# Linear attention and a multiplicative FFN on one core: full-height matmuls with block-diagonal kv, phi as a min, batch 0's attention ahead of the weights, and a new order on every engine

## The chip, the cores and the metric

One core of one Trainium2 chip. The metric is device time in microseconds of one execution, the median of several; the four runs of the kernel before lie within 0.6%, those of the changed kernel within 0.8%. The profile is of one further execution. It names the engines PE (TensorE), PEld (TensorE weight load), DVE (VectorE), ACT (ScalarE), POOL (GpSimd) and SP (SyncE). A ratio below is the mean time of one kernel's fast runs over that of the kernel before's fast runs of the same rounds, so not quite the ratio of the medians quoted beside it.

## The reference

```python
# q, k, v: (8 batches, 8 heads, 576 positions, 64), fp32
phi = lambda x: np.where(x > 0, x, np.exp(x) - 1.0) + 1.0
kv  = einsum('bhsd,bhse->bhde', phi(k), v)
z   = phi(k).sum(axis=2)
x   = einsum('bhsd,bhde->bhse', phi(q), kv) / (einsum('bhsd,bhd->bhs', phi(q), z)[..., None] + 1e-6)
x   = x.transpose(0, 2, 1, 3).reshape(4608, 512)
out = ((x @ w1) * (x @ w2)) @ w3 @ w_out     # 512 -> 1024 -> 1024 -> 512
```

Both kernels fold `w3 @ w_out` into one "fused weight" (wf) and cut the 4608 rows of x into nine chunks of 512. A chunk is eight a/b products (13.8 us of TensorE) and four outputs (6.9 us). 576 positions are 4 x 128 plus a remainder of 64.

## The kernel before

Every engine runs a fixed list of steps; the order of the lists is written out by hand. The parts that matter, shortened (`...` marks a cut):

```python
def phi_exp(name, b, g):                    # ScalarE
    nc.scalar.activation(out=e, in_=x, func=AF.Exp)
def phi_min(name, b, g):                    # VectorE
    nc.vector.tensor_scalar_min(out=e, in0=e, scalar1=1.0)
def phi_max(name, b, hp):                   # VectorE: max(x + 1, min(exp x, 1))
    nc.vector.scalar_tensor_tensor(out=out, in0=x, scalar=1.0, in1=e, op0=ALU.add, op1=ALU.max)

def kv_half(b, g):                          # 64-row matmuls, two halves side by side
    ...
    for n, (kk, vv, halves) in enumerate(steps):
        for r in halves:
            rows = slice(r * R, (r + 1) * R)
            nc.tensor.matmul(kvp[:, r, i * W:(i + 1) * W], kk[rows], vv[rows], ...)
    nc.scalar.copy(out=kvf, in_=kvp[:, 0, 0:2 * W])
    nc.vector.tensor_tensor(out=kvs[b]..., in0=kvf, in1=kvp[:, 1, 0:2 * W], op=ALU.add)
# numerators: 64-row matmuls, one per head (u) and head pair (hp)
nc.tensor.matmul(nd[0:n, u, hp * (D + 1):(hp + 1) * (D + 1)], w[rows], kvs[b][rows, hp, u, :], ...)
# transposes of q and x: on TensorE for the first batches, by DMA for q of batches 4 to 7, x of 2 and 4 to 7
nc.sync.dma_start(out=dst, in_=src, transpose=True)
```

## Time and profile before

| | kernel before |
|---|---|
| time, median | 261.6 us (260.9 to 262.5) |
| profiled span | 258.1 us, mean clock 0.999 |
| kv of batch 1, of batch 7 | 46.4 us, 193.1 us |
| all loads of the start (weights, batches 0 and 1) landed | about 56 us |

How to read it: the start is bound by loads. After that TensorE is full up to the end. The prediction shows the rows.

The table by stretches gives one line for 60 to 185 us, in which most of the attention of batches 2 to 7 is loaded and worked (in the kernel before, batch 7's comes after it); it is the line that all the rest is compared with. DMA share is the packets' time over that of 16 engines; it can pass 1, and is no proof of a bound by itself: from 50 to 75 us, in the prediction's table, it is 1.06 while TensorE is busy 24.95 of 25 us.

```profile
core 0: us, PE busy (x) PEld busy (x) DVE busy (x) ACT busy (x) POOL busy (x), PEclk, DMA share, GB/s
60.00:185.00 125.00, 124.47 (x943) 60.20 (x952) 104.52 (x282) 72.16 (x119) 2.45 (x4) 1.00 0.86 223
```

TensorE is busy 124.47 of 125 us at full clock, DMA at 0.86. The waits of TensorE in this stretch are an empty list.

### The profile page before, as it was taken

What the parts mean: (1) busy time and instruction counts of PE and PEld (TensorE: products, weight loads), DVE (VectorE), ACT (ScalarE), POOL (GpSimd) and SP (SyncE); (2) the same over time, 40 slices, a digit from 0 to 9 for tenths busy, and PEclk for the clock granted to TensorE, in tenths of its full rate; (3) what the DMA queues carried; (4) which work ended last, traced back from release to release, by engine and by line L of the source; (5) the groups of instructions that cost most, each with busy time, mean ns of one, the idle gap of its engine ahead of it and who ended that gap; (6) DMA issues with size and microseconds to landing.
All of it is one profiled execution on the core that took longest, in us unless ns stands there. A gap on an engine that the chain in (4) does not pass through costs nothing.

```text
span 258.1 us, 4507 instructions
## 1 busy us (share of the span) xinstructions
PE 237.4 (92%) x1656; PEld 116.2 (45%) x1673; DVE 167.9 (65%) x426; ACT 129.0 (50%) x205; POOL 21.1 (8%) x42
## 2 busy tenths in 40 slices
PE   1138999999999999999999999999999999999994
PEld 1124554545454454455444444444444444444442
DVE  0025787969978979997968589468866543423320
ACT  2048587858478664677353645726533203331421
POOL 8000765000101000000000000000000000000000
PEclk9999999999999999999999999999999999999999
DMA  6999999999898599939988975934980124003024
GB/s 100 200 257 378 316 229 245 208 334 307 302 291 250 87 340 215 307 104 253 211 193 245 369 160 123 248 99 131 218 220 26 34 57 124 0 37 125 3 82 163
DMA packets 70085, 48.98 MB, mean 190 GB/s; under 512 B 34416, under 2 KB 64368, under 8 KB 70064
## 3 DMA queue, kind: packets, MB, share of 16 engines
q1 hardware_dynamic: 63104, 42.54, 61.4%
q0 software_dynamic: 6816, 6.03, 14.1%
q8 instruction: 13, 0.21, 0.3%
q10 hardware_dynamic: 144, 0.13, 0.1%
q14 instruction: 8, 0.07, 0.1%
HBM read 38.80 MB, written 9.44 MB: 187 GB/s over the span
## 4 chain that ended last, share of the span: by engine, by line
PE 84%; DMA 8%; ACT 2%; SPq 1%; issue 1%; DVE 1%; DVEq 0%; POOLq 0%
PE a_ps L371 25%; PE b_ps L371 24%; PE o_ps L390 23%; DMA k<-in_k_dram 4%; DMA w3b<-in_moe_w_dram 4%; PE kvp L199 3%; PE wf_ps L464 3%; PE nd L265 3%; SPq L111 1%; PE tp L309 1%; PE w3p L454 1%; PE xtp L285 1%; PE o_ps L417 1%; DVE qj L162 1%; ACT e L137 0%
## 5 line engine op out<-in xcount | busy, mean ns | idle before, releaser
L371 PEld LDWEIGHTS <-w_sb 128*128 128x128 bf16 x576 | 54.2, 98 | 63.4 <-issue 0.5
L377 DVE TENSOR_TENSOR ab<-a_sb,b_ps 128x512 bf16<-128x512 f32 x72 | 49.0, 684 | 46.6 <-PE b_ps L371 35.4
L371 PE MATMUL a_ps<-xt,w_sb 128*128 128x512 bf16 x288 | 75.1, 380 | 0.1
L371 PE MATMUL b_ps<-xt,w_sb 128*128 128x512 bf16 x288 | 74.9, 379 | 0.0
L376 ACT COPY a_sb<-a_ps 128x512 f32<-128x512 f32 x72 | 41.9, 586 | 56.8 <-PE a_ps L371 55.6
L390 PE MATMUL o_ps<-wf_sb,ab 128*128 128x512 bf16 x266 | 63.2, 379 | 0.7
L390 PEld LDWEIGHTS <-ab 128*128 128x128 bf16 x280 | 26.7, 98 | 30.8
L393 ACT COPY o_sb<-o_ps 128x512 f32<-128x512 f32 x24 | 14.0, 583 | 30.7 <-PE o_ps L390 30.7
L162 DVE SCALAR_TENSOR_TENSOR kj<-k,e 128x256 bf16<-128x256 f32 x64 | 23.6, 417 | 0.1
L162 DVE SCALAR_TENSOR_TENSOR qj<-q,e 128x256 bf16<-128x256 f32 x64 | 23.4, 417 | 0.1
L141 DVE TENSOR_SCALAR e<-e 128x1024 bf16<-128x1024 bf16 x32 | 13.4, 420 | 14.2 <-ACT e L137 14.2
L137 ACT ACTIVATE e<-q 128x1024 bf16<-128x1024 f32 x16 | 16.7, 1058 | 9.3 <-DMA q<-in_q_dram 9.1
L454 PE MATMUL w3p<-ident,w3b 128*128 128x128 bf16 x64 | 6.1, 253 | 15.0 <-ACT w3t L455 8.0
L137 ACT ACTIVATE e<-k 128x1024 bf16<-128x1024 f32 x16 | 16.9, 1056 | 4.1 <-DMA k<-in_k_dram 2.7
L275 DVE TENSOR_TENSOR xn<-nd,r 128x512 bf16<-128x512 f32 x28 | 18.0, 686 | 0.0
L464 PE MATMUL wf_ps<-wo_sb,w3t 128*128 128x512 bf16 x61 | 16.7, 412 | 1.0 <-ACT w3t L455 0.8
L454 PEld LDWEIGHTS <-w3b 128*128 128x128 bf16 x64 | 4.9, 113 | 16.6 <-DMA w3b<-in_moe_w_dram 8.2
L393 DVE COPY o_sb<-o_ps 128x512 f32<-128x512 f32 x11 | 7.6, 688 | 6.4 <-PE o_ps L390 6.4
L171 ACT CAST vt<-v 128x1024 bf16<-128x1024 f32 x9 | 9.3, 1046 | 2.0 <-DMA v<-in_v_dram 2.0
L203 ACT COPY kvf<-kvp 128x260 f32<-128x260 f32 x14 | 5.3, 375 | 8.9 <-PE kvp L199 8.7
L464 PEld LDWEIGHTS <-w3t 128*128 128x128 bf16 x64 | 6.2, 104 | 7.8 <-issue 1.7
L199 PE MATMUL kvp<-vt,kj 64*128 64x130 bf16 x224 | 9.2, 217 | 0.0
(81 smaller groups left out, 163.5 us busy)
## 6 DMA issues: line engine op xcount, KB each, us to landing
out_dram<-o_sb SPq DMA_DIRECT2D x31, 256.0 KB, 3.2
k<-in_k_dram SPq DMA_DIRECT2D x7, 1024.0 KB, 8.6
q<-in_q_dram SPq DMA_DIRECT2D x7, 1024.0 KB, 8.2
v<-in_v_dram SPq DMA_DIRECT2D x6, 1024.0 KB, 7.4
w3b<-in_moe_w_dram POOLq DMA_DIRECT2D x8, 256.0 KB, 7.1
v<-in_v_dram SPq DMA_DIRECT2D x4, 512.0 KB, 8.5
w_sb<-in_moe_w_dram POOLq DMA_DIRECT2D x8, 256.0 KB, 11.3
out_dram<-o_sb SPq DMA_DIRECT2D x9, 128.0 KB, 2.4
```

The costliest lines, as they stand in the source:

```text
L137: nc.scalar.activation(out=e, in_=x, func=AF.Exp)
L141: nc.vector.tensor_scalar_min(out=e, in0=e, scalar1=1.0)
L162: nc.vector.scalar_tensor_tensor(out=out, in0=x, scalar=1.0, in1=e, op0=ALU.add, op1=ALU.max)
L199: nc.tensor.matmul(kvp[:, r, i * W:(i + 1) * W], kk[rows], vv[rows], start=(n == 0), stop=(n == (NJ if r == g else NJ - 1)))
L275: nc.vector.tensor_tensor(out=dst.rearrange("p (c u) e -> p u c e", u=2), in0=v4[:, :, :, 0:D], in1=r[0:n].unsqueeze(3).to_broadcast([n, 2 ...
L371: nc.tensor.matmul(ps, w[:, kc, f * P:(f + 1) * P], xt[:, 4 * c:4 * c + 4, kc, :], start=(kc == 0), stop=(kc == KC - 1))
L376: nc.scalar.copy(out=a_sb, in_=a_ps)
L377: nc.vector.tensor_mul(out=abs_[c][:, f, :], in0=a_sb, in1=b_ps)
L390: nc.tensor.matmul(o_ps, ab[:, f, m * P:(m + 1) * P], wf_sb[:, f, :], start=(f == 0), stop=(f == FC - 1))
L393: copy_of(alt)(out=o_sb, in_=o_ps)
L454: nc.tensor.transpose(tp[:, kc, :], raw["w3", i][:, kc * P:(kc + 1) * P], ident)
L464: nc.tensor.matmul(wfs[i], w3ts[i][:, kc, :], wo_sb[:, kc, :], start=(kc == 0), stop=(kc == FC - 1))
```

## The change

Intent: matmuls of one shape only (128 rows) so that TensorE never changes its tiling; less VectorE work for phi; an earlier first product, by loading batch 0 ahead of the weights. The diff is long; its core, cut:

```diff
-        nc.vector.tensor_scalar_min(out=e, in0=e, scalar1=1.0)
-            nc.vector.scalar_tensor_tensor(out=out, in0=x, scalar=1.0, in1=e, op0=ALU.add, op1=ALU.max)
+        nc.vector.tensor_scalar(out=d, in0=raw, scalar1=0.0, scalar2=1.0, op0=ALU.max, op1=ALU.add)
+        nc.vector.tensor_tensor(out=phi, in0=d, in1=e, op=ALU.min)      # min(exp x, max(x, 0) + 1)

-    def kv_half(b, g): ...                       # 36 matmuls of 64 rows a batch, copy and add
+    def kv(b, hp):                               # 5 matmuls of 128 rows a head pair
+        for j in range(NJ):
+            nc.tensor.matmul(dst, kj[:, hp, j]..., vt[:, j, 2 * hp:2 * hp + 2, :]..., ...)
+        nc.tensor.matmul(dst, kr[:, ...], vrz[:, b % 2, ...], ...)   # remainder, other batch's rows zero in vrz
+    def kc(b, g0, ng, r, eng):                   # the diagonal blocks alone go to kvb; the rest of kvb stays zero
+        copy_of[eng](out=kvb[b % 3][rows, ..., r, :], in_=ps["kv", b][rows, ..., r, :])
+    def na(b, jp, g):                            # numerators: 128 rows x 130 columns, two heads at once
+        nc.tensor.matmul(o[:, i, ...], sb["qt", b][:, hp, ...], kvb[b % 3][:, hp]..., start=True, stop=True)

+    # DMA transposes: q and x of batches 2 to 7 (six of each)
-    ORDER = """ L0.3 E0 I0 M0.0 x0.2 N0.3 E1 X0.0 w0 ...      (w3 and w_out first)
+    ORDER = """ ... lr:k,0,s ld:k,0,0,4,s lr:v,0,s ld:v,0,0,4,s ld:q,0,0,4,s ...   (batch 0, w1/w2, w_out, w3, batch 1)
```

In the step names of the new order, `ld`/`lr` are loads (whole batches and remainders), `x`, `t`, `m` the three steps of phi, `kv`/`kc` kv and its copies, `na`/`nd` numerators and division, `qt`/`qc` and `xp`/`xc` transposes on TensorE with their copies, `qd` and `xd` transposes by DMA, `f`, `ac`, `ab` the a/b products, `o`, `oc`, `st` output, copy, store, `w3t`, `wf` the fused weight.

> **What bounds the kernel now.** I read the page's table by slices first, then the chain that ended last, the table by stretches, the order of time on TensorE, and last the landings of the DMAs.
>
> The page:
>
> ```profile
> span 258.1 us, 4507 instructions
> PE 237.4 (92%) x1656; PEld 116.2 (45%) x1673; DVE 167.9 (65%) x426; ACT 129.0 (50%) x205; POOL 21.1 (8%) x42
> PE   1138999999999999999999999999999999999994
> DVE  0025787969978979997968589468866543423320
> PEclk9999999999999999999999999999999999999999
> DMA  6999999999898599939988975934980124003024
> PE 84%; DMA 8%; ACT 2%; SPq 1%; issue 1%; DVE 1%; DVEq 0%; POOLq 0%
> ```
>
> TensorE is full from the fourth slice (a slice is 6.45 us) to the end at an ungated clock. Only the first three slices and the tail are not TensorE; there the DMA row is at 9. So the kernel is a start of some 30 us, a solid block of matmuls, and a tail. The table by stretches says the same:
>
> ```profile
> core 0: us, PE busy (x) PEld busy (x) DVE busy (x) ACT busy (x) POOL busy (x), PEclk, DMA share, GB/s
> 20.00:30.00 10.00, 9.11 (x61) 4.89 (x59) 7.24 (x18) 8.36 (x11) 4.71 (x8) 1.00 1.10 368
> 50.00:75.00 25.00, 24.95 (x180) 12.67 (x180) 22.65 (x60) 16.95 (x29) 1.22 (x2) 1.00 1.06 301
> 75.00:100.00 25.00, 24.89 (x207) 12.46 (x207) 20.73 (x56) 16.16 (x27) 1.22 (x2) 1.00 0.94 218
> 100.00:125.00 25.00, 24.89 (x227) 12.38 (x227) 23.55 (x70) 16.06 (x27) 0.00 (x0) 1.00 0.90 234
> ```
>
> From 50 to 125 us TensorE is 99.6% busy although VectorE is 89% busy (66.9 of 75) and DMA 0.90 to 1.06: both have little room beneath TensorE.
>
> A busy PE may hide gaps, so I took start-to-start times from the timeline. An a/b product is 8 matmuls in 1.73 us, 216 ns each; a 128x128 transpose costs 57.5 ns. The small attention products:
>
> ```profile
> 74.66 1.03 PE L371 MATMUL b_ps<-xt,w_sb 128*128 128x512 bf16 x4
> 75.62 0.40 PE L199 MATMUL kvp<-vt,kj 64*128 64x130 bf16 x8
> 76.36 0.44 PE L199 MATMUL kvp<-vt,kj 64*128 64x130 bf16 x9
> 76.59 0.22 PE L199 MATMUL kvp<-vr,kr 64*128 64x130 bf16 x1
> 76.74 1.04 PE L371 MATMUL a_ps<-xt,w_sb 128*128 128x512 bf16 x4
> ```
>
> The b product's last matmul should hand over at 74.66 + 4 x 0.216 = 75.52; kv starts at 75.62, and hands back at 76.74. So the 36 half-height matmuls of one batch cost 1.12 us (31 ns each, two halves side by side) plus 0.10 us of change. 16 half-height numerator products cost 0.35 + 0.10 us. From 30.0 us to the last matmul's start at 254.06 these steps sum to 224.1 us without a hole. The end is therefore (when the block starts) + (its content) + (tail).
>
> **What the Trainium skill says.** "TensorEngine Tiling (Array Packing)", Key Properties: changing the tiling mode drains TensorE, and tiles work in parallel. The trace agrees with both: 0.10 us per change, 31 ns per half-height matmul. "VectorE: DVE Perf Modes", the perf-mode tier table: tensor_tensor on bf16 in SBUF runs at 2x, tensor_scalar on fp32 in SBUF at 2x, fp32 tensor_tensor at 1x. The trace: the fp32-to-bf16 cast of 1024 took 702 ns, bf16 tensor_scalar of 1024 420 ns, fused fp32 add/max of 256 417 ns (1x). "DMA: Bandwidth & Descriptors", Issuing engines are not separate DMA queues: all issuers share 16 engines, so moving loads to GpSimd's queue brings no bandwidth. The trace has about the same ceiling whoever issues (368 GB/s above; w1/w2 alone some 365 GB/s of fp32 read).
>
> **Part by part.**
>
> *Full-height matmuls.* kv: 8 batches x 20 matmuls, numerators 8 x 20, each 130 wide, estimated at 58 ns (the transposes' 57.5 plus two columns): 1.16 us each a batch. Before: 1.22 for kv and about 1.25 for the numerators. That is 0.15 us a batch, 1 us in all; half-height was already nearly as quick. Q transposes on TensorE fall from 64 to 32: 1.8 us less. The kv sum of halves (ACT copy 375 ns and DVE add 423 ns) becomes two copies.
>
> *phi.* Per half tensor (1024 columns) VectorE did a min, 0.42, and four fused ops of 0.37 effective (23.6 us / 64): about 1.85 us. Now: one fp32 tensor_scalar, about 0.62 effective, and two bf16 mins of 512, about 0.37 each if at 2x: 1.36. 32 halves save about 15 us of VectorE, none of it on TensorE's path.
>
> *Content.* w1/w2 products 576 x 216 = 124.3; output 62.2; fused weight 64 x 216 = 13.8; w3 transposes 3.7; kv 9.3; numerators 9.3; q and x transposes 3.7. Sum 226.3 us.
>
> *The new start.* This is where the change earns. Before, w3 and w_out came first, and batch 0's kv ran at 29.2. Now k, q, v of batch 0 go alone (3.4 MB), then w1/w2 (4.2 MB read), w_out and w3 (6.3 MB), then batch 1. First data at about 2.3 us (before's first 64 KB landed at 3.18). At 380 GB/s with the 256 B rows batch 0 is in at 11.7. w1/w2 wait for q, then at 365 GB/s run 12.8 to 24.3. w_out and w3 at about 340 (what the first 20 us of before averaged) end at 42.8. Batch 1 is in at 52.2.
>
> TensorE: batch 0's chain exp, min, kv, transposes, division, transposes, with before's durations (1.06 exp, 0.69 copy, 1.0 for a division), ends at about 18. The first products wait for weight pairs at about 16, 19, 22, 24.5; chunk 0 is done at 32. The fused weight takes 17.5 us plus about 3 waiting for w3. Batch 1's v lands at 52.5, is cast, and its kv starts at about 53.7. By then 36.0 us of the 226.3 are done, by adding up the new order. So 190.3 are left: TensorE could end at 244.0, against 254.35 before. The tail was 3.7; now the last tile is copied whole (0.69 against 0.42) and stored in two issues of 0.6 from one queue: 4.4. Span 248.4; time was span plus 3.55: **251.9 us if nothing stalls**.
>
> *The middle.* The new order wants batch 7's kv at 130 us of TensorE work; before it came at 193 us, and after it only 96 us of pure products remain, now 40% of the kernel. From batch 1's kv to batch 7's are 95 us of TensorE. VectorE beneath: six batches at about 12.1 (2.5 tensor_scalar, 3.0 min, 0.7 rest, 4.6 division, 1.3 copies), 3 left of batch 1, 29 products at 0.62: 94 us. DMA beneath: six batches at 9.9 = 59, q and x transposes by DMA 22 (about 2.25 each of the large, from 2048 packets), 16 stores 10: 91 us. All three are nearly full, for longer than before's 89%. With DMA never idle, the DMA-transposed q of batches 3, 4 and 5 would land 2.8, 3.7 and 1.6 us after TensorE wants them. There are also spots with four numerator units in a row on two PSUM tiles, each waiting for a 1 us division. I charge 4.6 us of stalls: **256.5 us**.
>
> **The rivals.**
> - *The start is all that counts.* For: before's tuned order kept TensorE full over an 89% VectorE. Then 251 to 253.
> - *The middle becomes bound by VectorE or DMA.* For: 94 and 91 of 95 us, queues in order, stores and transposes ahead of loads on one queue. Before's DMA moved only 218 to 301 GB/s there. Against: loads are issued well ahead, which keeps DMA full. 10 to 14 us of stalls: 262 to 266.
> - *The early start is lost again.* Weights only from GpSimd might move at 310 GB/s, or batch 0's chain take 25 us. As before got its 6 MB of w3 and w_out during the wait for batch 0, the order is partly a swap. v of batch 1 would land at 56 to 57: 259 to 261.
> - *The min stays at 1x* because its output is written in 64-element runs: 64 x 0.27 = 17 us more VectorE, which lands in the second rival.
>
> **Range and chances.** Mean stalls 4.6, with an uncertainty of about 4 (0 to 13), and about 2.5 on the start. 2% faster is 256.4, right at my centre. Predicted 256.5 us, 250.5 to 263; faster 0.48, same 0.47, slower 0.05. Slower needs over 266.9, that is 15 us of stalls, which only a middle limited at 87% would give.
>
> **What would show it right or wrong.** Right start: batch 0's kv near 8 to 13 us, first a product near 17 to 19, batch 1's kv near 54. Full height: no 0.10 us hand-over, kv matmuls 57 to 59 ns apart. phi: bf16 min of 512 near 0.41 us, tensor_scalar near 0.68. Middle: VectorE and DMA above 90% from 55 to 150 us with some 3 to 8 us of holes on TensorE before numerators or kv; TensorE solid after batch 7's kv. The prediction is wrong if batch 1's kv comes after 58 us, or if holes in the middle sum to over 10 or under 1 us.

## The result, and the profile after

| | before | after |
|---|---|---|
| time, median | 261.6 us | 291.1 us (289.6 to 292.0) |
| ratio of fast runs | 1 | 1.112 (1.108 to 1.117) |
| profiled span, mean clock | 258.1 us, 0.999 | 287.5 us, 0.958 |
| kv of batch 1, of batch 7 | 46.4, 193.1 us | 59.1, 184.4 us |

It is 11% slower, far out of the range. The page of the changed kernel, the lines that answer to those in the prediction (slices of 7.19 us; the last two are the chain that ended last, by engine and by line):

```profile
span 287.5 us, 3967 instructions
PE 249.9 (87%) x1456; PEld 127.7 (44%) x1456; DVE 165.0 (57%) x354; ACT 117.3 (41%) x175; POOL 21.1 (7%) x38
PE   7567999997898847996793998989999999999993
PEclk9779999999799995999799799999999999999999
DMA  6999999599999999999799377439109100002423
PE 59%; DMA 21%; DVE 11%; SPq 3%; ACT 3%; issue 2%; DVEq 0%; ACTq 0%
```

Before, the PE row was solid from the fourth slice on, the clock row all 9, and the chain 84% PE. Now the PE row has dents from the tenth slice to the twenty-seventh, the clock row has 7s and a 5 in them, and DMA holds 21% of the chain. The stretch from 60 to 185 us, as above:

```profile
60.00:185.00 125.00, 102.84 (x617) 51.17 (x614) 92.90 (x216) 62.89 (x91) 0.00 (x0) 0.93 0.99 235
```

21.6 us less TensorE in the same time, a clock of 0.93, and DMA at 0.99 on the mean over 125 us (1.09 up to 150 us, 0.73 after it). VectorE is busy 74%, less than before's 84%, so it is not full. The largest waits of TensorE in this stretch (who waited, for whom, us in total, times, longest):

```profile
PE ndr L315 <- DVE kvb L250: 4.6, 1, 4.6
PE a_ps L382 <- DMA xt<-xn: 3.9, 1, 3.9
PE nd L290 <- DVE xn L298: 2.7, 3, 1.9
PE nd L290 <- ACT kvb L250: 2.4, 1, 2.4
PE xtp L333 <- DVE xn L298: 2.2, 2, 1.6
```

Two of them read closely. First the product that waited 3.9 us for x of batch 3, on SyncE's queue (start, us the issue took, what was issued):

```profile
118.17 0.40 SPq L130 DMA_DIRECT2D q<-in_q_dram  x1
118.67 2.38 SPq L130 DMA_DIRECT2D k<-in_k_dram  x1
121.16 7.80 SPq L275 DMA_TRANSPOSE qt<-q  x1
129.01 0.57 SPq L130 DMA_DIRECT2D v<-in_v_dram  x1
129.64 5.38 SPq L346 DMA_TRANSPOSE xt<-xn  x1
```

Batch 3's last division group was finished at 116.4 us (the matmuls of the four groups stand from 105.0 to 108.6). Its transpose was issued only at 129.64, behind loads and behind a q transpose whose issue alone took 7.80 us on the full DMA. Its own issue took 5.38 us, it landed at 138.43, and the product started at 138.47.

Then the 4.6 us wait that is put down to VectorE (VectorE's own timeline; in brackets its idle time and what ended it):

```profile
151.44 0.69 DVE L219 CAST vt<-v 128x1024 bf16<-128x1024 f32 x1
156.75 0.43 DVE L202 TENSOR_SCALAR tr<-k32r 128x512 bf16<-128x512 f32 x1 [4.62 <-DMA k32r<-in_k_dram]
157.41 0.42 DVE L214 TENSOR_TENSOR kr<-tr,er 128x512 bf16<-128x512 bf16 x1 [0.23 <-ACT er L196]
157.75 0.42 DVE L250 CAST kvb<-kvp 64x260 bf16<-64x260 f32 x1
```

VectorE was not slow, it stood still. The kv sums of batch 5 were ready at 150 us, and their copy is 0.42 us of work; but it is listed behind a phi step for the pair of batches 6 and 7, and that step's 128 KB load, issued at 145.84 us, landed at 156.73. The Trainium skill ("TensorE: Matmul & The Clock Gate", Architectural detail) calls VectorE's queue strictly first in, first out, and the trace agrees: the head of the list held the copy for 4.6 us. So this wait too is a late transfer, one link further back.

For the comparisons below I added up, from the timeline, how much TensorE time was *lost* by a given moment: the moment, less the undisturbed start-to-start times of all real matmuls started before it (matmuls of zeros count as nothing; a matmul at half clock loses its extra time). For the kernel before, the 0.1 us hand-overs between tilings and a few missing records count as lost too, so its row is some 7 us too high at the end.

| lost by (us) | 60 | 80 | 100 | 120 | 160 | 200 | end |
|---|---|---|---|---|---|---|---|
| before | 24.7 | 25.5 | 26.3 | 27.8 | 30.2 | 32.5 | 33.8 |
| after | 23.7 | 28.9 | 32.3 | 41.2 | 53.1 | 56.9 | 56.9 |

By 60 us the two are level: the new start has won 1 us. Nearly all of the rest, 33 us, is lost between 60 and 185 us.

### The profile page after: what moved, and what is told of

It reads as the page before. It is cut to its first block, busy times and chain, and to the rows that moved or that the text cites. A ratio compares the mean times of both kernels' runs of the same rounds, so it can differ in the third digit from the quotient of the medians.

```text
span 287.5 us, 3967 instructions
## 1 busy us (share of the span) xinstructions
PE 249.9 (87%) x1456; PEld 127.7 (44%) x1456; DVE 165.0 (57%) x354; ACT 117.3 (41%) x175; POOL 21.1 (7%) x38
## 4 chain that ended last, share of the span: by engine, by line
PE 59%; DMA 21%; DVE 11%; SPq 3%; ACT 3%; issue 2%; DVEq 0%; ACTq 0%
PE a_ps L382 18%; PE b_ps L382 17%; PE o_ps L407 13%; PE wf_ps L370 5%; DMA qt<-q 4%; DMA k32r<-in_k_dram 4%; DMA q32r<-in_q_dram 4%; DMA q<-in_q_dram 3%; DMA xt<-xn 3%; DVE xn L298 2%; SPq L130 2%; DMA xt<-xnr 2%; DVE t L174 2%; PE kvp L240 1%; DVE k L182 1%
## 5 line engine op out<-in xcount | busy, mean ns | idle before, releaser
L401 DVE TENSOR_TENSOR ab<-a_sb,b_ps 128x512 bf16<-128x512 f32 x72 | 49.4, 685 | 61.5 <-PE b_ps L382 55.2
L413 ACT COPY o_sb<-o_ps 128x512 f32<-128x512 f32 x21 | 12.2, 583 | 27.5 <-PE o_ps L407 27.1
L290 PE MATMUL nd<-kvb,qt 128*128 128x130 bf16 x128 | 12.2, 229 | 7.3 <-DVE xn L298 3.7
L240 PE MATMUL kvp<-vt,k 128*128 128x130 bf16 x128 | 11.8, 228 | 4.8 <-DVE vt L219 3.9
L370 PE MATMUL wf_ps<-wo,w3t 128*128 128x512 bf16 x64 | 14.3, 379 | 0.5 <-ACT w3t L364 0.5
L290 PEld LDWEIGHTS <-qt 128*128 128x128 bf16 x128 | 8.9, 101 | 12.9 <-DVE xn L298 5.1
L182 DVE TENSOR_TENSOR q<-t,e 128x512 bf16<-128x512 bf16 x32 | 12.4, 418 | 3.2 <-DMA qt<-q 2.1
L240 PEld LDWEIGHTS <-k 128*128 128x128 bf16 x128 | 9.4, 102 | 8.1 <-DVE vt L219 4.1
L182 DVE TENSOR_TENSOR k<-t,e 128x512 bf16<-128x512 bf16 x32 | 12.4, 418 | 0.4
L174 DVE TENSOR_SCALAR t<-k 128x1024 bf16<-128x1024 f32 x16 | 11.0, 701 | 1.7 <-DMA k<-in_k_dram 1.6
L174 DVE TENSOR_SCALAR t<-q 128x1024 bf16<-128x1024 f32 x16 | 11.2, 704 | 0.9 <-DMA q<-in_q_dram 0.8
L115 PE MATMUL kvp<-zero 128*128 128x252 bf16 x61 | 10.5, 350 | 1.2 <-DVE zero L99 1.2
```

What stands on the lines that cost most here:

```text
L174: nc.vector.tensor_scalar(out=d[:, 0:nh * W], in0=raw[n, b][:, h0 * W:(h0 + nh) * W], scalar1=0.0, scalar2=1.0, op0=ALU.max, op1=ALU.add)
L182: nc.vector.tensor_tensor(out=d[:, hp].rearrange("p j u d -> p u j d"), in0=ts[n, b, h0][:, s].rearrange("p (u j d) -> p u j d", u=2, j=NJ ...
L240: nc.tensor.matmul(dst, kj[:, hp, j].rearrange("p u d -> p (u d)"), vt[:, j, 2 * hp:2 * hp + 2, :].rearrange("p h e -> p (h e)"), start=(j ...
L290: nc.tensor.matmul(o[:, i, a * PW:(a + 1) * PW], sb["qt", b][:, hp, j * P:(j + 1) * P], kvb[b % 3][:, hp].rearrange("p u e -> p (u e)"), s ...
L370: nc.tensor.matmul(o, sb["w3t", i][:, c, :], sb["wo"][:, c, :], start=(c == 0), stop=(c == FC - 1))
L401: nc.vector.tensor_mul(out=d[:, f, :], in0=sb["a", c, f], in1=ps["b", c, f])
```

## The experiments

Theory at the outset: the new order wants all loads and DMA transposes much earlier, DMA cannot keep up, and TensorE waits. Rivals: VectorE is the bound; the late start costs it; single transfers stand in the wrong place of the one queue; the halved clock is a cost of its own; the changed arithmetic costs it. Runs are in the fast state except where said (one of the four of n6_sametr, 284.7 us, and one of n11_half, 273.1 us, count as slow and are not in the ratios); every wrong result was on purpose.

### n1_warm: the start

```diff
-    kv:0,1 kv:0,0 wk:0,20 x:q,0,0,4 t:q,0,0,4 kc:0,0,1,0,v kc:0,0,1,1,v
+    kv:0,1 kv:0,0 x:q,0,0,4 t:q,0,0,4 kc:0,0,1,0,v kc:0,0,1,1,v wk:0,20
```

> The change with its twenty warm-up matmuls moved from before to behind the two copies of batch 0's first kv (the copies waited 3.0 us for these matmuls, which share the PSUM tile). If that wait is what made batch 0 late, batch 1's kv starts 2 to 4 us earlier than 59.1 and the time falls by 2 to 4 us from 291; if the start is bound by DMA or the middle takes it all back, the time stays within 1 us.

289.5 us (ratio 1.108, 1.100 to 1.115); before 261.5. Batch 1's kv came 1.3 us earlier (57.8), and 26.4 us of holes after 60 us stayed. So the wait for the warm-up matmuls is not the cause; what else the start costs, this run does not test.

### n2_copy and n3_pool: transposes, and whose queue

n2_copy makes each DMA transpose a plain copy of the same size; n3_pool issues the loads of batches 2 to 7 from GpSimd, so that transposes and stores have SyncE's queue to themselves.

```diff
-        nc.sync.dma_start(out=d.rearrange("p c (j t) -> p (c j) t", t=P), in_=..., transpose=True)     # n2_copy
+        nc.sync.dma_start(out=d.rearrange("p c t -> p (c t)"), in_=...)
-    ... ld:k,2,0,8,s ... ld:v,2,0,8,s ld:q,2,0,8,s ...                                                  # n3_pool
+    ... ld:k,2,0,8,g ... ld:v,2,0,8,g ld:q,2,0,8,g ...
```

> The change with each DMA transpose replaced by a plain DMA copy of the same bytes (wrong result on purpose; 4 KB pieces in place of 256 B ones), all else and all waits kept. DMA theory (transposes and loads together fill the DMA engines from 60 to 158 us, TensorE waits for landings): the holes after 59 us fall from about 25 to under 10 us and the time to 260 to 272. VectorE theory: the holes stay, time 284 to 290. Queue theory (SyncE's one queue in order): part of it, since issues get shorter too.

> The change with all loads of batches 2 to 7 issued by GpSimd, so that transposes and stores on SyncE's queue no longer stand in front of them (correct result, same bytes). Queue theory: time falls by 8 us or more, to under 283. DMA theory: same bytes through the same 16 engines, time within 4 us of 291.

n2_copy: 275.3 us (1.053), 16 us back. That is outside the 260 to 272 us of the DMA theory, and some 16 us of holes stayed where under 10 were expected: the transposes are a large part, not all. n3_pool: 307 to 324 us; three of its four runs count as slow, so there is no ratio, but even the fastest, 307.0 us, is 15 us over the slowest of the changed kernel. In the profiled run, a slow one of 324 us, a q transpose took 15 us to issue and landed at 101.09, with a hole of 15.5 us on TensorE behind it:

```profile
76.26 15.28 SPq L275 DMA_TRANSPOSE qt<-q  x1
```

So taking the loads out of the queue does not free the transposes. A likely reading, from this one trace, is that the loads were all let go at once, and the transposes got a smaller share of a full DMA (a share of 1.02 from 60 to 185 us, but 199 GB/s in place of 235). That agrees with the Trainium skill ("DMA: Bandwidth & Descriptors", Issuing engines are not separate DMA queues): another issuer brings no bandwidth.

### n4_dve2: VectorE

```diff
+        for _ in range(2 if b > 1 else 1):
             nc.vector.tensor_scalar(out=d[:, 0:nh * W], ..., op0=ALU.max, op1=ALU.add)
```

> The change with the fp32 tensor_scalar of phi done twice for batches 2 to 7 (24 more of 0.70 us, about 15 to 17 us more VectorE work, same result). VectorE theory: time rises by 12 us or more. DMA theory: VectorE has slack beneath the waits, time rises by under 6 us.

293.3 us (1.122), 2 us more than the changed kernel, for some 16 us more of VectorE. VectorE is not the bound.

### n11_half and n14_beforehalf: fewer bytes, in both kernels

Of batches 2 to 7 only heads 0 to 3 are loaded, and used twice; the compute steps stay the same. The same cut in both kernels (short form):

```diff
+        if b >= 2: nh = 4                                            # load half
-   in_=raw[n, b][:, h0 * W:(h0 + nh) * W]
+   in_=raw[n, b][:, s * W:(s + nh) * W]          # s = 0 if b >= 2 else h0
```

> The changed kernel, but of batches 2 to 7 only heads 0 to 3 of q, k, v are loaded and used twice (wrong result on purpose): 9.4 MB less of the 50.6 MB that DMA moves, nothing else changed. If late transfers (full DMA from 60 to 158 us) cost the time after 80 us, the DMA row falls below 9 there, the holes of 4 us at 138 and 158 us vanish, and the time is 270 to 279 us; what is left is the bare attention of batches 1 and 3. If the order's own waits (attention steps one after the other) cost all of it: 286 us or more.

> The control to n11_half: the kernel before with the same cut, of batches 2 to 7 only heads 0 to 3 loaded and used twice (wrong result on purpose; 9.4 MB less). The same cut gave the changed kernel 21 us. If late transfers bind the changed kernel because of its order, and not every kernel of this program, the kernel before gains less than 3 us: 258 to 261 us. If DMA binds the kernel before as well: 245 to 253 us.

n11_half: 269.6 us, 269.0 on the mean of its three fast runs (1.031, 1.023 to 1.039): about 22 us back, just better than expected. n14_beforehalf: 260.9 us, ratio 0.999 (0.996 to 1.003): nothing. The stretch from 60 to 185 us, of n11_half, then of n14_beforehalf:

```profile
60.00:185.00 125.00, 116.30 (x737) 59.92 (x736) 106.04 (x249) 67.66 (x100) 0.00 (x0) 1.00 0.82 183
```

```profile
60.00:185.00 125.00, 124.47 (x943) 60.20 (x952) 104.60 (x283) 73.89 (x121) 2.45 (x4) 1.00 0.58 151
```

The changed kernel gets 13.5 us of TensorE back as DMA falls from 0.99 to 0.82, and its clock is whole again. The kernel before stays at 124.47 to the last digit while its DMA falls from 0.86 to 0.58: it had never waited for these bytes. What is left of TensorE's waits in n11_half is this, its three largest:

```profile
PE nd L292 <- DVE xn L300: 2.3, 4, 1.0
PE xtp L335 <- ACT e L170: 1.6, 1, 1.6
PE a_ps L384 <- DVE xt L342: 0.9, 1, 0.9
```

Both long waits of the changed kernel are gone, the one put down to VectorE as well. So late transfers are the larger part, and they are a matter of this order and its choice of transposes.

### n5_oldorder, n6_sametr, n7_qpe: the order, and what goes over DMA

n5_oldorder keeps all of the changed arithmetic and the new start (as in n1_warm), but from batch 1 on the steps stand as in the kernel before, with its choice of what goes over DMA (q of batches 4 to 7, x of 2 and 4 to 7). n6_sametr and n7_qpe keep the new order and take q (and x) transposes from DMA to TensorE.

```diff
-    ORDER = """ ... (the new order from batch 1 on)                       # n5_oldorder
+    ORDER = """ ... (steps of the kernel before from batch 1 on, translated; e bufs 4, t 3, er 2, ldr 5, ab 2)
-    ... qd:2 ... qd:3 ... xd:3 ...                                         # n6_sametr; n7_qpe: qd:2 to qd:7
+    ... qt:2,0 qc:2,0,v qt:2,1 qc:2,1,a ...
```

> All of the changed kernel's arithmetic (full-height matmuls, block-diagonal kv, new phi) and its new start (batch 0's attention first), but from batch 1 on the steps stand in the order of the kernel before, with its choice of which transposes go over DMA (q of batches 4 to 7, x of 2 and 4 to 7). Buffers: e 4, t 3, the remainder loads 5, ab 2. Theory (the new order asks for all batches' loads and transposes too early, DMA is full from 60 to 158 us, TensorE gets holes and half clock): the holes after 60 us fall from 26 to under 8 us, half clock nearly gone, and the time is 254 to 262 us. Rival A (the arithmetic or the phi itself costs the time, by VectorE or PSUM hand-overs): it stays above 278 us. Rival B (the late start costs it): stays near 280 us with few holes.

> The changed kernel with its own order, but q of batches 2 and 3 and x of batch 3 transposed on TensorE as in the kernel before (the DMA transposes are then the same ones as before's). Tells the choice of what goes over DMA from the order. If DMA's load between 60 and 158 us is the bound, 1.5 MB less of transposes (three of some 2 to 5 us each at full DMA) gives back 5 to 12 us for 2.8 us more TensorE work: 280 to 287 us. If the order alone is the cause whatever goes over DMA: 289 to 295 us.

> The changed kernel with all q transposes of batches 2 to 7 on TensorE (6 fewer DMA transposes of 512 KB; 96 transposes of 58 ns = 5.6 us more on TensorE, 12 copies more on VectorE and ScalarE). Theory (DMA transposes landing late behind loads): q no longer waits for DMA, holes after 60 us fall from 26 to about 12 us, time 276 to 285 us. Rival (it isn't the DMA transposes of q): 294 to 298 us, as the work added.

n5_oldorder: 282.5 us (1.086), not the 254 to 262 expected. n6_sametr: 281.7 us (1.079); n7_qpe: 286.5 us (1.099), the first as the DMA theory had it, the second 1.5 us over its range: less DMA helps, but not by itself. The miss of n5_oldorder taught the most:

| lost by (us) | 60 | 80 | 100 | 120 | 160 | 200 | end |
|---|---|---|---|---|---|---|---|
| n5_oldorder | 25.6 | 34.4 | 36.5 | 44.3 | 46.5 | 47.4 | 49.4 |
| n6_sametr | 22.3 | 29.5 | 35.5 | 40.0 | 42.7 | 46.5 | 47.5 |

After 120 us n5_oldorder loses 5 us where the changed kernel loses 16: there the old order mends it. But from 50 us (20.9 lost) to 80 us it lost 13.5. One reason lies in the start that it shares with the changed kernel. Both starts, before's and the new one, have their loads complete at about 56 us. The kernel before has then done part of chunk 0, and runs batch 1's attention (46.4 us) between chunk 0's products. The new start has used all of chunk 0 and all of the fused weight by 58.6 us (56.1 in n5_oldorder), so batch 1's attention stands *bare*: each short step waits for the copy or division of the step before, with only chunk 0's four outputs to put between.

That is not all of it, though. The largest hole, 4.6 us, is n5_oldorder's own:

```profile
56.16 0.59 ACT L375 CAST wf_sb<-wf_ps 128x512 bf16<-128x512 f32 x1 [5.45 <-PE wf_ps L370]
56.77 2.00 ACT L168 ACTIVATE e<-k 128x1024 bf16<-128x1024 f32 x2
59.63 1.03 ACT L219 CAST vt<-v 128x1024 bf16<-128x1024 f32 x1
60.71 0.59 PE L240 MATMUL kvp<-vt,k 128*128 128x130 bf16 x4 [4.59 <-ACT vt L219]
```

ScalarE's list has the last fused weight's cast ahead of batch 1's exp, though k had landed at 49.8 us. The changed kernel has no such wait. The bare steps after it add five holes of 0.5 to 1.0 us, and the clock was halved from 59.9 to 73.6 us. And of the 7.8 us that n5_oldorder lost between 100 and 120, the cause is one place in SyncE's queue:

```profile
80.32 0.53 SPq L130 DMA_DIRECT2D q<-in_q_dram  x1
95.61 1.20 SPq L351 DMA_TRANSPOSE xt<-xnr  x1
96.90 1.30 SPq L138 DMA_DIRECT2D k32r<-in_k_dram  x2
106.11 0.63 ACT L196 ACTIVATE er<-q32r 128x512 bf16<-128x512 f32 x1 [8.04 <-DMA q32r<-in_q_dram]
```

A transpose that waited for its input stood at the head of the queue for 14.8 us, and DMA's share fell to 0.00 from 85 to 95 us with five loads behind it. So the rival of single transfers in the wrong place is real, in this run.

### n8_fill, n9_fillnew, n10_best, n13_mend: a start that keeps something to fill with

```diff
-    lo, l3:0 .. l3:7, then batch 1's loads; all of wf, then batch 1's attention
+    lo, l3:0 .. l3:3, batch 1's loads, l3:4 .. l3:7; batch 1's attention between wf:4 .. wf:7      # n8_fill (old order after), n9_fillnew (new order after)
+    the transpose of the first remainder x (xdr:0) behind the loads that it held up                # n8_fill only
+    l3:0 .. l3:5 first; w3t one step ahead; kc after all four kv of a batch                        # n10_best
+    batch 2's loads gated on l3:6; its phi spread among f:1,0 .. f:1,4                             # n13_mend
```

> As n5_oldorder, but batch 1's loads go ahead of the second half of the w3 blocks, and batch 1's attention stands among the fused-weight products (it stood after all of them); the transpose of the first remainder x leaves the place in SyncE's queue where it held the loads up from 80 to 95 us. The theory by now: by 60 us the changed kernel has done as much TensorE work as the one before (both have lost 24 us by then, both have their start's loads complete at 55.6 us), but it has spent the work that could fill gaps (chunk 0's products and the fused weight), so batch 1's attention stands bare: each step waits for the one before, and the gaps bring the half clock. If so, hiding batch 1's attention removes the 14 us that n5_oldorder lost between 50 and 80 us, and some of the 8 us between 100 and 115: 257 to 268 us. Rival (whatever the place, the attention's steps or the DMA cost this time): 278 us or more.

> The new start of n8_fill with the changed kernel's own order and own DMA transposes from batch 2 on: with the changed kernel, n5_oldorder and n8_fill it makes a square of two starts and two orders of the rest. If bare attention of batch 1 is what the new order's stretch from 60 to 80 us loses, some 5 to 8 us come back: 281 to 286 us; the loss after 100 us (24 us in the changed kernel) stays, as the transposes over DMA and the loads behind them are untouched. If the loss is all in the start: 262 to 272 us. If the start has nothing to do with it: 288 to 293 us.

> n8_fill with three more repairs: six of the eight w3 blocks load ahead of batch 1 (q last), each w3 transpose stands a step ahead of its product, and in every later batch the two kv copies stand after all four head pairs (n8_fill made the second pair wait 0.84 us for the first pair's copy, four times). All of the changed kernel's arithmetic is in it, and the order after batch 1 is that of the kernel before. If the arithmetic is harmless and the order made all the difference, the start's loss falls from 32 to 24 to 26 us and the rest's from 6 to 3 us: 260 to 267 us, within 2.5% of the kernel before. If it stays at 271 us or more, something of the arithmetic costs time beyond what the order explains.

> n10_best with batch 2's loads let go earlier (after the seventh w3 block, not after q of batch 1) and batch 2's phi and transposes spread among the first five products of chunk 1 (they stood ahead of the first). n10_best lost 6.9 us from 70 to 80 us there, to one hole of 3.3 us, one of 0.9 us and 6.8 us at half clock. If that, and not the changed arithmetic, is what is left, the time falls to 263 to 267 us. If it stays at 270 us or more, the arithmetic is suspect.

| | time | ratio | lost by 60 | 80 | 100 | 120 | 160 | end |
|---|---|---|---|---|---|---|---|---|
| n8_fill | 272.8 us | 1.045 | 29.4 | 32.0 | 34.6 | 34.6 | 36.1 | 37.9 |
| n9_fillnew | 290.8 us | 1.116 | 29.5 | 31.4 | 34.5 | 41.0 | 53.6 | 58.1 |
| n10_best | 271.5 us | 1.038 | 23.6 | 31.2 | 34.6 | 34.7 | 35.3 | 36.1 |
| n13_mend | 271.4 us | 1.038 | 27.5 | 29.2 | 36.5 | 38.0 | 39.4 | 41.4 |

n8_fill and n9_fillnew have the same start and differ in the rest, its order and its choice of transposes: 18 us. With the old order the rest loses 6 us from 80 us to the end; with the new one, 27. n9_fillnew shows that the filled start alone buys nothing (it expected 281 to 286): the loss from 60 to 80 us fell from 5.2 to 1.9 us, and 5.8 us more were lost before 60; after it the losses are again those of the changed kernel. Nor does the filled start explain n8_fill's 10 us over n5_oldorder: by 100 us it is only 1.9 us ahead, and 7.8 us come between 100 and 120, where its queue is mended.

```profile
60.00:185.00 125.00, 119.46 (x764) 62.24 (x762) 95.64 (x221) 70.01 (x110) 0.00 (x0) 1.00 0.87 221
```

That is n8_fill: clock whole, DMA 0.87, as in the kernel before. n10_best was expected at 260 to 267 and came at 271.5; n13_mend at 263 to 267, and came at 271.4. Each mended the place it aimed at, and lost the time at the next one: n10_best at batch 2's q (a hole of 3.3 us at 73.4 us and 6.8 us at half clock), n13_mend at batch 2's kv and numerators (holes of 0.9 to 1.4 us at 85 to 88 us and 6.8 us at half clock). A hand-made start that never runs out of filling was not reached, and no reordering here beats the kernel before. By the words of both expectations, 270 us or more puts the changed arithmetic under suspicion. The table speaks against it: from 120 us to the end n10_best, with all of that arithmetic, loses 1.4 us. Its excess lies before 100 us, in the start and the first batches.

### n12_zeros: is the halved clock a cost of its own?

```diff
+    def z(c, f, n):       # n matmuls of zeros into the PSUM tile of the next a product
+        for _ in range(n): nc.tensor.matmul(t, zero[:, 0:P], zero, start=True, stop=True)
+    ... z:1,2,7 xp:1,1,1 ... z:2,0,11 na:3,0,1 ... z:3,7,18 f:3,7 ... z:3,5,21 nar:5
```

> The changed kernel with matmuls of zeros in its own known holes (71, 72, 73, 105, 108, 109, 111, 138 and 158 us), each filled to about nine tenths of what it measured: TensorE is kept busy, no wait is taken away. The traces show 17 us at half clock after such holes, which is 8.5 us of lost work. If the halved clock comes from the holes and is a cost of its own, the half-clock stretches after 60 us vanish and the time falls to 281 to 286 us. If the clock was only the image of the holes and no cost, or the zeros get in the way: 289 to 294 us.

296.7 us (1.135): slower, and outside both expectations. Three of the four half-clock stretches after 60 us vanished (at 73, 107 and 138 us), and yet the time lost by 140 us was 47.7 us, against 46.9 in the changed kernel with them. So up to there no cost of the clock's own shows. Either TensorE would only have waited longer for the same transfers, or the zeros took what the clock gave; the run cannot tell. After 150 us the zeros got in the way (they waited for a PSUM tile until 159.7 us, 5.5 us), so for the end of the stretch the run says nothing.

### n15_phi and n16_kvfull: parts of the arithmetic alone, in the kernel before

```diff
-        nc.vector.tensor_scalar_min(out=e, in0=e, scalar1=1.0)                     # n15_phi
+        nc.vector.tensor_scalar(out=t, in0=x, scalar1=0.0, scalar2=1.0, op0=ALU.max, op1=ALU.add)   # t: over x
-            nc.vector.scalar_tensor_tensor(out=out, in0=x, scalar=1.0, in1=e, op0=ALU.add, op1=ALU.max)
+            nc.vector.tensor_tensor(out=out, in0=t, in1=e, op=ALU.min)
-                kv_half(b, i)                                                      # n16_kvfull
+                kv_copy(b, i, kv_full(b, i), i == 1)
```

> One part alone: the kernel before with the new phi, min(exp x, max(x, 0) + 1), in place of max(x + 1, min(exp x, 1)); the max part is written over the loaded tile, as there is no room for another. It takes some 15 us from VectorE, none of it on the path that sets the end. If the arithmetic is harmless: 259.5 to 262 us, VectorE some 12 to 15 us less busy. If VectorE's room matters in the kernel before: 255 to 258 us. If the new phi is what costs the changed kernel time: over 265 us.

> Another part alone: the kernel before with kv of batches 1 to 7 by full-height matmuls (20 a batch in place of 36 half-height ones), and two plain copies in place of copy and add. Work on TensorE nearly unchanged (some 1.1 to 1.2 us a batch in both forms): 259.5 to 262 us. If full height saves what the prediction said, a share of 1 us at most, within the noise. If it costs: over 263 us.

n15_phi: 260.0 us (0.994, 0.989 to 0.999), with VectorE at 154.6 us busy, 13.3 less. The new phi is harmless, and worth half a per cent at most by itself (the verdict at 2% is "same"). n16_kvfull: 266.2 us (1.019, 1.014 to 1.025), 5.5 us slower: the case "if it costs" of its expectation. Its timeline shows why (the second line is the remainder, which this version leaves at 64 rows):

```profile
76.60 0.39 PE L220 MATMUL kvp<-vt,kj 128*128 128x130 bf16 x4
76.92 0.23 PE L224 MATMUL kvp<-vr,kr 64*128 64x130 bf16 x1
77.08 0.40 PE L220 MATMUL kvp<-vt,kj 128*128 128x130 bf16 x4
...
78.56 0.61 PE L372 MATMUL a_ps<-xt,w_sb 128*128 128x512 bf16 x2
```

From 76.60 to 78.56, 1.96 us a batch, where the kernel before needs 1.12: the tiling changes twice for each head pair. 0.84 us x 7 batches are 5.9 us, enough for all of the 5.5. The Trainium skill ("TensorEngine Tiling (Array Packing)", Key Properties) says that a change of mode drains TensorE; here such a pair costs 0.2 us. The changed kernel avoids it by zero-padding the remainder to 128 rows, and pays 1.13 us a batch, from 148.85 to 149.98 us:

```profile
148.85 0.39 PE L240 MATMUL kvp<-vt,k 128*128 128x130 bf16 x4
149.08 0.22 PE L243 MATMUL kvp<-vrz,kr 128*128 128x130 bf16 x1
...
149.98 1.03 PE L382 MATMUL a_ps<-xt,w_sb 128*128 128x512 bf16 x4
```

So by these durations the full-height form is neutral when it is complete. The change's own full-height form was not run by itself in the kernel before; that it is neutral there is argued, not shown.

## Why the prediction was wrong

- *Full-height matmuls: right.* 1.13 us of kv a batch against 1.16 predicted, no hand-over; about nothing won.
- *phi: right.* bf16 min of 512 took 0.42 us, the fp32 tensor_scalar of 1024 0.70; and n15_phi confirms that VectorE's gain is nearly worthless for the time.
- *The start: 5 us too early.* v of batch 1 landed at 55.6 us, not 52.5, and its kv ran at 59.1, not 53.7. The second half of q landed at 14.1 us (all of batch 0 was predicted in at 11.7), the weights were gated on it, and the last of w1/w2 came at 29.5 where 24.3 was predicted. Batch 0's kv was right (10.2 us, 8 to 13 predicted), but the first a product came at 25.3, not 17 to 19. The win of 10 us (244.0 against 254.35) shrank to at most the 1 us of the table. The third rival had the landing nearly right (56 to 57 us).
- *"DMA beneath: six batches at 9.9 = 59, q and x transposes by DMA 22, 16 stores 10: 91 us."* This is the term that failed. In the trace, between 60 and 185 us, DMA moved 17,552 packets of 1 KB at a mean of 55 ns, 29,696 of 256 B at 26 ns and 1,822 of 2 KB at 108 ns. Over 16 engines that is 59.8 + 49.0 + 12.3 us, and with 2.2 of 4 B packets some 123 us. The views behind it:

```profile
DMA packets 50392, 29.44 MB, mean 235 GB/s; under 512 B 31008, under 2 KB 48560, under 8 KB 50382
qt<-q SPq DMA_TRANSPOSE x5, 5.9
qtr<-qr SPq DMA_TRANSPOSE x4, 3.6
xt<-xn SPq DMA_TRANSPOSE x3, 7.8
xt<-xnr SPq DMA_TRANSPOSE x3, 3.9
```

  The 256 B packets are 8 large transposes of 2,048, 7 small ones of 512, and 19 remainder loads of 512, together the 29,696. By purpose, at the same mean for all of them: loads 75.9 (59.8 of 1 KB rows and 16.1 of 256 B remainders) where I had 59; transposes 32.9 where I had 22; stores 12.3 where I had 10. My 2.25 us for a large transpose are 17.6 ns a packet, the median here (18 ns); the mean is 26 ns, and was 24 in the kernel before, where it could have been read. The order leaves these transfers 95 us of TensorE work. From kv of batch 1 to kv of batch 7 the changed kernel took 125.3 us (59.1 to 184.4), close to DMA's 123. The match is in part chance: DMA is full to about 156 us and has gaps after it. Before, the same span was 146.7 us (46.4 to 193.1), and DMA had room.
- *"I charge 4.6 us of stalls."* Follows from the last point: 26.3 us of holes after 60 us, and 17 us at half clock besides. The second rival ("the middle becomes bound by VectorE or DMA") had the mechanism, and its size, 10 to 14 us, failed with the same sum; n4_dve2 and n11_half show it was DMA, not VectorE. Both signs of being wrong that the prediction named came true: batch 1's kv after 58 us, and over 10 us of holes in the middle.
- *Not in the prediction at all:* that the new start uses up the work that could be laid between the steps of batch 1's attention. With halved loads the changed kernel is still some 8 us slower than the kernel before, and its waits are of attention's steps for each other (n11_half's list). But only 3.6 us of its loss falls between 60 and 80 us, at batch 1; n9_fillnew mended that stretch and won nothing, and most of n8_fill's gain came from elsewhere. So this part is argued, and small. Also missing was the clock, but n12_zeros found no cost of its own up to 140 us.

Settled by runs: about 22 us of the 30 are late transfers (n11_half against n14_beforehalf). How much of that is the order and how much the three more large transposes is not settled: taking those three back to TensorE gave some 9 us (n6_sametr), order and choice together 18 (n8_fill against n9_fillnew). Left open: the other 8 are read from traces of waits, but no reordering brought them back; and whether the full-height form costs a microsecond in some other place.

## What to carry to other kernels

Before moving work earlier, add up for the shortened stretch what each shared resource must deliver, with packet durations measured under load and small packets counted for themselves: here 123 us of DMA had been squeezed under 95 us of TensorE. Where a queue or a list is worked in order, look at what stands behind each step that has to wait: one transpose at the head of a queue left DMA idle for 10 us in n5_oldorder. Keeping work that depends on nothing for the chains of short steps looks right from the traces, but no run here won by it. And when a wait is put down to an engine that is not full, look at that engine's own timeline: the head of its list may be waiting for a load.

## What the Trainium skill lacked or had wrong

- "TensorE: Matmul & The Clock Gate", Why this matters for your kernels: asks for no idle gaps above some 3 us between bursts. In the changed kernel three gaps of 1.7, 0.8 and 1.0 us within 4 us (70.9 to 73.2) came with 3.4 us at half clock from 72.8 on. In n11_half the same three gaps (1.7, 0.8 and 1.0 us at 70.6 to 72.9) did not; the page's free-running window may be why, which no run here tests. (Another section of the page does warn of frequent short idle times, without a figure.)
- "Advanced Engine Details and Errata", X-Bar Transpose (TRN2): transposes are said to be as fast as plain DMAs. Here a 512 KB transpose goes in 2,048 packets of 256 B; these took 26 ns on the mean (remainder loads' included), 155 GB/s over 16 engines, where the 1 KB rows of the loads ran at 300, and still 21 ns from 185 to 200 us with no such load beside them; and replacing transposes by plain copies gave 16 us (n2_copy).
- No page says that a transpose holds its issuing queue the longer the fuller DMA is ("DMA: Bandwidth & Descriptors" has one issue time for transposes pushed tile by tile, without the load): 1.7 us at 172.5 us, where DMA had gaps, 5.4 and 7.8 us under load in the changed kernel, 15 us in n3_pool; all that stands behind it waits.
- "TensorEngine Tiling (Array Packing)", Key Properties: gives no cost for a change of mode. Here 0.10 us before a block of 64-row matmuls, and 0.84 us a batch where a 64-row matmul stands among 128-row ones (n16_kvfull).
